# Windowed attention with a top-2 mixture of experts: a ring of nine slots for the values, three buffers for the turned values, and gate logits in half-width matmuls

## The chip, the cores and the metric

The kernel runs on one core of one Trainium2 chip. The metric is the device time of one execution in microseconds (us), from start to end on that core; lower is better. Times here are medians of several executions. One execution was also taken with the hardware profiler, and all rows below come from it.

## What is computed

The input is q, k and v of shape (8 batches, 8 heads, 576 positions, 64 features). Each position attends to itself and to the 63 positions before it. The attention output, seen as 4608 rows of 512 features, goes through a noisy top-2 gate and eight experts, each of two matmuls (512 to 1024, relu, 1024 to 512):

```python
mask = (rel >= 0) & (rel < window)              # window = 64
scores = np.where(mask, scale * q @ k.T, -1e9)
attn = softmax(scores);  x = attn @ v           # x: 4608 rows of 512
logits = x @ w_gate
noisy = logits + np.log1p(np.exp(x @ w_noise)) * noise
top2 = the two largest of the 8 experts, with softmax weights
out[row] += weight * (relu(x[row] @ w1[e]) @ w2[e])   # for both experts
```

All is in float32. The kernel never multiplies the attention output by the gate matrices. It multiplies v by them first, and lets the attention average the results: the gate logits of a key are 16 more value columns beside its 64 features.

## The kernel before, in words

**Two phases.** The attention phase has 36 steps, numbered j (NT = 36). Step j is block i = j // 4 of 64 positions of a pair of batches bp = j % 4. The expert phase follows, expert by expert; its first matmuls begin while the last steps of attention still run. The loop over j (lines 1104 to 1162) is written out by hand, and that order is the order of every engine's queue: nothing is rescheduled. Each engine works its own queue in order, and so does SyncE's queue, which issues the transfers.

**One step of the loop.** In the order of the code, with the engine that does it:
- `norm_a(j-3)` (lines 385 to 389): ScalarE copies the sums of the softmax (L388), VectorE takes the reciprocal (L389).
- `scores(j)` (L318; L320 in the first four steps): TensorE, 16 matmuls in 64x64 tiles of the array.
- `soft_a(j)` (L328): ScalarE copies a part of the scores into the tile `t`. In the first four steps GpSimd fills `t` instead (L330).
- `soft_b(j-1)` (L346): ScalarE takes the exponential and writes `p`.
- `pv(j-2)` (L378): TensorE, 32 matmuls in 64x64 tiles (16 in the first four steps), with the values of this block and of the block before. Then SyncE is told to load the values of step j+2 (`load_v`, L131).
- `place_slots(j-2)` (L608): TensorE, a few small bf16 matmuls of the routing.
- `norm_b(j-3)` in two halves (L399): ScalarE, eight scaled copies.
- `soft_max(j)`, `soft_max2(j)` (L336, L341, L342): VectorE merges the scores and takes the maximum, GpSimd subtracts it.
- `transp(j-1)` (L354): TensorE turns `p`, four transposes.
- `logits(j)` (lines 282 to 288): TensorE, the gate logits of the 128 keys of step j; then SyncE is told to load the turned values of step j+2 (`load_vt`, L137).
- `apply_mask(j-1)` (L359): VectorE.
- `logits_copy(j)` (lines 290 to 295): ScalarE moves the logits from PSUM beside the values.
- `gate(j-3)` (L416), and a share of the routing's small instructions, which come from a list on VectorE, ScalarE and GpSimd.

**The values.** `VW` (line 112) is one tile for each of the four pairs of batches, with two slots, i % 2. A slot holds four groups of value columns, which a transfer brings, and a fifth group with the gate logits, which ScalarE writes. `pv(j)` reads the slots of steps j and j-4. The load for step j+4 writes the slot that `pv(j)` reads as the block before. GpSimd zeroes the fifth groups once (L185).

**The turned values.** `VT` (L136) has two buffers. The load for step j+2 takes the buffer that `logits(j)` reads.

**The logits.** For each of four groups q of 128 rows of turned values, one matmul takes 128x128 weights (64 keys of each of two heads) and 64 moving columns, of which each half of the keys needs 32. The copy takes the right 32 for each half of the partitions, so there are two of it:

```python
nc.tensor.matmul(p[:, q * 64:q * 64 + 64], lhsT=x[:, q, :], rhs=wgx_sb[:, g], ...)
for a in range(2):                      # L292
    nc.scalar.activation(VW[bp][h, i % 2, 4, ...], VG[h, 0]...[:, :, a], AF.Copy)
```

**The start.** GpSimd works through masks, the zeroing of L185 and the constants of the routing (lines 428 to 458 and 637) in order, and only then fills `t` for step 0 (L330).

Of the kernel before, what the change touches and what calls it, by code (L numbers as in the profile page):

```python
# [8 lines left out]
F32 = mybir.dt.float32  # L9
# [4 lines left out]
AF = mybir.ActivationFunctionType  # L14
# [6 lines left out]
NP = B // 2  # L21
# [67 lines left out]
def tile_kernel(ctx, tc, qT, kT, vx, vT, wgx, noise, w1, w2, out):  # L89
    nc = tc.nc  # L90
# [14 lines left out]
    acon = at.enter_context(tc.tile_pool(name="acon", bufs=1))  # L105
    ld = at.enter_context(tc.tile_pool(name="ld", bufs=2))
    wk = at.enter_context(tc.tile_pool(name="wk", bufs=2))
# [1 line left out]

    KW = acon.tile([128, NP, 2, H, 64], F32)  # L110

    VW = [acon.tile([128, 2, 5, 2, 4, 17], F32, name=f"vw{j}") for j in range(NP)]
    QC, VT = {}, {}

    def load_q(j):
# [12 lines left out]

    def load_v(j):
        i, bp = divmod(j, NP)  # L130
        nc.sync.dma_start(VW[bp][:, i % 2, 0:4], vx[bp, i])  # L131


    def load_vt(j):
        i, bp = divmod(j, NP)
        VT[j] = ld.tile([128, 4, 128], F32, name="vt", bufs=2)  # L136
        nc.sync.dma_start(VT[j], vT[bp, i])  # L137

    for j in range(2):
# [1 line left out]
    wgx_sb = acon.tile([128, 2, 64], F32)  # L141
    nc.sync.dma_start(wgx_sb, wgx)
    load_vt(0)
    load_v(0)
    load_vt(1)
    load_qk(2)
    load_v(1)
    load_k(3)

# [3 lines left out]
    idle = ps.tile([128, 512], F32, name="ps_g")  # L153
# [19 lines left out]
    nc.vector.tensor_scalar(mcur, mprev, -1.0, 1.0, op0=OP.mult, op1=OP.add)  # L173

    maskT = acon.tile([128, 2, 2, 64], F32)
    other = acon.tile([128, 2, 64], F32)
    o3 = ones.rearrange("p (u r) -> p u r", u=2)
    nc.gpsimd.affine_select(maskT[:, 0], o3, pattern=[[0, 2], [1, 64]], base=0, channel_multiplier=-1,
                            compare_op=OP.is_ge, fill=0.0)
# [2 lines left out]
    nc.vector.tensor_copy(maskT[64:128, 0], other[64:128])  # L182
    nc.vector.tensor_scalar(maskT[:, 1], maskT[:, 0], -1.0, 1.0, op0=OP.mult, op1=OP.add)
    for v in VW:
        nc.gpsimd.memset(v[:, :, 4], 0.0)  # L185


    noise_sb = consts.tile([128, NT, E], F32)
# [88 lines left out]
        return lag([(w2s[:, f], W2["h"][:, f], W2["l"][:, f]) for f in (0, 4, 1, 5, 2, 6, 3, 7)])  # L277


    VG = idle[:, 0:256].rearrange("p (n c) -> p n c", n=1)  # L280

    def logits(j):
        p = VG[:, 0]
        x = VT.pop(j)
        for u in range(2):
            for g in range(2):
                q = u * 2 + g
                nc.tensor.matmul(p[:, q * 64:q * 64 + 64], lhsT=x[:, q, :], rhs=wgx_sb[:, g], start=True, stop=True)

    def logits_copy(j):  # L290
        i, bp = divmod(j, NP)
        for a in range(2):  # L292
            h = slice(a * 64, a * 64 + 64)
            nc.scalar.activation(VW[bp][h, i % 2, 4, :, :, 0:16].rearrange("p u (g x) e -> p (u g) x e", x=2),
                                 VG[h, 0].rearrange("p (k a x e) -> p k a x e", a=2, x=2, e=16)[:, :, a], AF.Copy)

    ST, T, P, TP, PT, XT = {}, {}, {}, {}, {}, {}

# [67 lines left out]
    def pv(j):  # L366
        i, bp = divmod(j, NP)
        o = aps.tile([128, 2, 512], F32, name="ps_o", bufs=2)
        OT[j] = o
        PO[j] = o[:, :, 0:340].rearrange("p a (k d) -> p a k d", d=85)  # L370
        pt, v = PT.pop(j), VW[bp]
        for g in range(2):
            for x in range(2):
                for w in range(2 if i else 1):
                    for a in range(2):
                        for u in range(2):
                            pa = slice(a * 64, a * 64 + 64)
                            nc.tensor.matmul(PO[j][u * 64:u * 64 + 64, a, g * 2 + x, :],  # L378
                                             lhsT=pt[pa, w, u * 2 + g, x * 64:x * 64 + 64],
                                             rhs=v[pa, (i + w) % 2, :, u, g * 2 + x, :],  # L380
                                             start=(w == 0), stop=(w == 1 or not i))
        if j + NP < NT:
            load_v(j + NP)
# [64 lines left out]
    for k in (1, 2, 4, 8, 16, 32):  # L448
        n = min(k, NT - k)
# [654 lines left out]
    for j in range(NT + 3):  # L1104
# [17 lines left out]
        if W1G // 2 - 4 <= j < W1G // 2 + 4:  # L1122
            k = j - W1G // 2 + 4
# [5 lines left out]
        ahead(2)  # L1129
        drain(rate(1))  # L1130
        on(pv, j - 2)
        on(place_slots, j - 2)
        if PACED <= j < NT - 3:
# [12 lines left out]
        on(transp, j - 1)  # L1146
        ahead(2)
        on(logits, j)
        if j < NT - 2:
            load_vt(j + 2)  # L1150
        blanks(j)
        on(norm_b, j - 3, 1)
        on(apply_mask, j - 1)
        drain(rate(2))
        on(logits_copy, j)
        ahead(2)
        on(gate, j - 3)
# [14 lines left out]
    d, z, v, y = ([mps.tile([128, 512], F32, name=f"ps_{x}{q}") for q in range(k)] for x, k in zip("dzvy", (2, 3, 1, 1)))  # L1172
# [188 lines left out]
```

## Time and profile before

| what | us |
|---|---|
| median of 3 runs (lowest, highest) | 998.04 (997.68, 999.22) |
| the profiled execution | 997.35 |
| its span, first to last instruction | 995.3 |
| busy in the span: TensorE | 956.3 |
| VectorE | 689.9 |
| ScalarE | 525.9 |
| GpSimd | 320.1 |

The profiled execution is 0.69 us under the median. A busy time is the time in which the engine had at least one instruction at work. TensorE's matmuls overlap each other, so TensorE may be counted busy while it does less than it could. PE is TensorE's matmuls and PEld its weight loads, DVE is VectorE, ACT ScalarE, POOL GpSimd, and SPq the queue on SyncE. An arrow such as `L354 <- ACT p L346` names what ended a wait; `<- issue` means that the profile shows nothing that the engine waited for. A float32 matmul of the code appears as two records on PE and two on PEld.

### The profile page before, as it was taken

The numbers are of one execution on the slowest core, as the hardware profiler recorded it, in microseconds if no ns is written. First come the engines' busy times: TensorE is split into PE (matmuls) and PEld (weight loads), VectorE is DVE, ScalarE is ACT, GpSimd is POOL, SyncE is SP. The second block draws the span as 40 slices with busy tenths as digits, with TensorE's granted clock in tenths as the row PEclk, the third lists the DMA queues.
The fourth block names the chain that finished last, engine by engine and source line by source line (L and its number), as shares of the span: only waits on it lengthen the run. The fifth ranks groups of instructions, "written<-read, shape, count | busy, mean of one in ns | idle before, by whom it ended". The sixth has DMA issues, their size and how long they took to land. (4 is left out here: it accounts for less than half of the span.)

```text
span 995.3 us, 21900 instructions
## 1 busy us (share of the span) xinstructions
PE 956.3 (96%) x8408; PEld 858.2 (86%) x8408; DVE 689.9 (69%) x1728; ACT 525.9 (53%) x1346; POOL 320.1 (32%) x442
## 2 busy tenths in 40 slices
PE   8788888999999999999999999999999999999996
PEld 8777787888879888989898989898989898989895
DVE  5688898763786777767766786668666867686730
ACT  4888877522455545544554455445544554455531
POOL 5346546122322414040414141413131323241303
PEclk9999999999999999999999999999999999999999
DMA  9989997894649456854584458454945494647304
GB/s 326 365 270 314 287 294 273 271 263 119 153 89 267 81 130 132 252 73 120 116 265 70 125 115 267 60 134 87 283 63 143 73 266 89 149 93 206 48 1 56
DMA packets 107810, 168.93 MB, mean 170 GB/s; under 512 B 13424, under 2 KB 57712, under 8 KB 105904
## 3 DMA queue, kind: packets, MB, share of 16 engines
q1 hardware_dynamic: 90544, 126.96, 41.7%
q0 software_dynamic: 17152, 40.48, 21.9%
q8 instruction: 68, 1.11, 0.5%
q14 instruction: 46, 0.38, 0.1%
HBM read 110.08 MB, written 57.32 MB: 168 GB/s over the span
## 5 line engine op out<-in xcount | busy, mean ns | idle before, releaser
L966 POOL DMA_INDIRECT out_dram<-xg,los x70 | 111.9, 1598 | 427.5 <-ACT xh L774 124.3
L900 ACT ACTIVATE hb<-tq 128x288 fp32r<-128x288 f32 (+1 forms) x168 | 76.9, 458 | 143.9 <-DVE tq L919 143.7
L1038 PE MATMUL ps_d<-w2h,hb 128*128 128x512 f32 x392 | 152.9, 390 | 0.0
L1039 PE MATMUL ps_d<-w2l,hb 128*128 128x512 f32 x392 | 152.8, 390 | 0.0
L1040 PE MATMUL ps_d<-w2h,hb 128*128 128x512 f32 x392 | 152.7, 390 | 0.0
L919 DVE TENSOR_TENSOR tq<-ps_z,tq 128x288 f32<-128x288 f32 (+1 forms) x168 | 79.2, 472 | 89.0 <-PE ps_z L890 88.5
L888 PE MATMUL ps_z<-xh,WH 128*128 128x288 f32 (+1 forms) x448 | 137.5, 307 | 0.9
L889 PE MATMUL ps_z<-xl,WH 128*128 128x288 f32 (+1 forms) x448 | 135.2, 302 | 0.0
L890 PE MATMUL ps_z<-xh,WL 128*128 128x288 f32 (+1 forms) x448 | 135.2, 302 | 0.0
L904 DVE SCALAR_TENSOR_TENSOR hb<-tq,hb 128x320 fp32r<-128x320 f32 (+2 forms) x168 | 75.6, 451 | 37.5 <-ACT hb L900 35.2
L888 PEld LDWEIGHTS ps_z<-xh,WH 128*128 128x128 f32 x448 | 84.0, 188 | 5.5 <-DVE tq L919 3.7
L1040 PEld LDWEIGHTS ps_d<-w2h,hb 128*128 128x128 f32 x392 | 73.6, 188 | 15.6
L1038 PEld LDWEIGHTS ps_d<-w2h,hb 128*128 128x128 f32 x392 | 73.6, 188 | 14.0
L1039 PEld LDWEIGHTS ps_d<-w2l,hb 128*128 128x128 f32 x392 | 73.6, 188 | 13.8
L889 PEld LDWEIGHTS ps_z<-xl,WH 128*128 128x128 f32 x448 | 84.1, 188 | 1.1
L890 PEld LDWEIGHTS ps_z<-xh,WL 128*128 128x128 f32 x448 | 84.1, 188 | 0.0
L698 POOL DMA_INDIRECT xg<-xrows,lxs x70 | 69.0, 986 | 23.2 <-issue 22.6
L782 ACT ACTIVATE xh<-tq 128x512 fp32r<-128x512 f32 (+1 forms) x70 | 42.7, 610 | 61.9 <-DVE tq L778 60.5
L235 DVE TENSOR_TENSOR WL<-ws,WH 128x512 fp32r<-128x512 f32 x112 | 67.2, 615 | 6.6 <-ACT WH L243 6.5
L399 ACT ACTIVATE x<-ps_o,r 128x80 f32<-128x80 f32 x288 | 67.0, 350 | 7.5 <-DVE r L389 7.2
L378 PE MATMUL ps_o<-vw,pt 64*64 64x85 f32 x2176 | 49.9, 235 | 12.7 <-issue 8.2
L342 POOL TENSOR_TENSOR t<-t,mx 128x512 f32<-128x512 f32 x36 | 38.8, 1078 | 70.8 <-DVE mx L341 49.2
(242 smaller groups left out, 2347.0 us busy)
## 6 DMA issues: line engine op xcount, KB each, us to landing
ws<-in_w_dram SPq DMA_DIRECT2D x14, 2048.0 KB, 11.5
xs<-xg SPq DMA_DIRECT2D x63, 256.0 KB, 3.4
vw<-in_vx_dram SPq DMA_DIRECT2D x36, 272.0 KB, 4.5
out_dram<-zero SPq DMA_DIRECT2D x38, 256.0 KB, 4.6
qc<-in_qT_dram SPq DMA_DIRECT2D x36, 256.0 KB, 4.8
KW<-in_kT_dram SPq DMA_DIRECT2D x36, 256.0 KB, 4.9
vt<-in_vT_dram SPq DMA_DIRECT2D x36, 256.0 KB, 4.6
xrows<-x SPq DMA_DIRECT2D x36, 256.0 KB, 4.9
```

What stands on the lines that cost most here:

```text
L235: eng.tensor_tensor(l, x, h.bitcast(F32), op=OP.subtract)
L698: nc.gpsimd.indirect_dma_start(out=XG[e, c, q][:m], out_offset=None, in_=X[:DUMP + seen.get((e, c), NT) * 128], in_offset=bass.IndirectOff ...
L888: nc.tensor.matmul(p[:, :n], lhsT=WH[:, a, k, w], rhs=xh[:, b, k, :n], start=first and k == 0, stop=False, **free)
L889: nc.tensor.matmul(p[:, :n], lhsT=WH[:, a, k, w], rhs=xl[:, b, k, :n], start=False, stop=False, **free)
L890: nc.tensor.matmul(p[:, :n], lhsT=WL[:, a, k, w], rhs=xh[:, b, k, :n], start=False, stop=(k == 1), **free)
L900: nc.scalar.activation(hh[:, f, a:b], src, AF.Relu)
L904: nc.vector.scalar_tensor_tensor(hl[:, f, a:m], src[:, :m - a], 0.0, hh[:, f, a:m].bitcast(F32), op0=OP.max, op1=OP.subtract)
L919: nc.vector.tensor_tensor(t, a[:, :n], t, op=OP.add)
L966: s = nc.gpsimd.indirect_dma_start(out=out[:(2 + seen.get((e, c), NT)) * 128], out_offset=bass.IndirectOffsetOnAxis(ap=LT[e, c][1][q][:m], ...
L1038: nc.tensor.matmul(p, lhsT=h, rhs=w2h[:, f, :], **a)
L1039: nc.tensor.matmul(p, lhsT=h, rhs=w2l[:, f, :], start=False, stop=False)
L1040: nc.tensor.matmul(p, lhsT=l, rhs=w2h[:, f, :], **b)
```

## The change

The values get nine tiles of one slot each, used in turn by j. The turned values get a third buffer. Each logits matmul is cut in two: 64 keys as weights (128x64) and the 32 columns that they need, written to the half of the partitions where those keys belong; one copy then moves all of it. The small mask `other`, used once at the start, moves into a buffer of `t`. The program uses 4,256 more bytes of each partition (one slot more of 2,720, one turned buffer more of 2,048, less 512 for `other`).

```diff
-    VW = [acon.tile([128, 2, 5, 2, 4, 17], F32, name=f"vw{j}") for j in range(NP)]
+    VW = [acon.tile([128, 5, 2, 4, 17], F32, name=f"vw{j}") for j in range(2 * NP + 1)]
...
-        nc.sync.dma_start(VW[bp][:, i % 2, 0:4], vx[bp, i])
+        nc.sync.dma_start(VW[j % len(VW)][:, 0:4], vx[bp, i])
...
-        VT[j] = ld.tile([128, 4, 128], F32, name="vt", bufs=2)
+        VT[j] = ld.tile([128, 4, 128], F32, name="vt", bufs=3)
...
-    other = acon.tile([128, 2, 64], F32)
+    other = wk.tile([128, 8, 64], F32, name="t")[:, 0:2]
...
     for v in VW:
-        nc.gpsimd.memset(v[:, :, 4], 0.0)
+        nc.gpsimd.memset(v[:, 4], 0.0)
...
-    VG = idle[:, 0:256].rearrange("p (n c) -> p n c", n=1)
+    VG = idle[:, 0:128].rearrange("p (n c) -> p n c", n=1)
...
-                nc.tensor.matmul(p[:, q * 64:q * 64 + 64], lhsT=x[:, q, :], rhs=wgx_sb[:, g], start=True, stop=True)
+                for a in range(2):
+                    h = slice(a * 64, a * 64 + 64)
+                    nc.tensor.matmul(p[h, q * 32:q * 32 + 32], lhsT=x[:, q, h], rhs=wgx_sb[:, g, a * 32:a * 32 + 32],
+                                     start=True, stop=True)
...
-        for a in range(2):
-            h = slice(a * 64, a * 64 + 64)
-            nc.scalar.activation(VW[bp][h, i % 2, 4, :, :, 0:16].rearrange("p u (g x) e -> p (u g) x e", x=2),
-                                 VG[h, 0].rearrange("p (k a x e) -> p k a x e", a=2, x=2, e=16)[:, :, a], AF.Copy)
+        nc.scalar.activation(VW[j % len(VW)][:, 4, :, :, 0:16].rearrange("p u (g x) e -> p (u g) x e", x=2),
+                             VG[:, 0].rearrange("p (k x e) -> p k x e", x=2, e=16), AF.Copy)
...
-        pt, v = PT.pop(j), VW[bp]
+        pt, v = PT.pop(j), [VW[(j - w * NP) % len(VW)] for w in range(2)]
...
-                                             rhs=v[pa, (i + w) % 2, :, u, g * 2 + x, :],
+                                             rhs=v[w][pa, :, u, g * 2 + x, :],
```

## Rows read from the trace of the kernel before

**Rows 1.** The page: busy time of each engine, and the queue of instructions.

```profile
PE 956.3 (96%) x8408; PEld 858.2 (86%) x8408; DVE 689.9 (69%) x1728; ACT 525.9 (53%) x1346; POOL 320.1 (32%) x442
...
q8 instruction: 68, 1.11, 0.5%
```

**Rows 2.** Busy time by stretch of the attention phase (stretch, length, each engine's busy us).

```profile
core 0: us, PE busy (x) PEld busy (x) DVE busy (x) ACT busy (x) POOL busy (x), PEclk, DMA share, GB/s
5.70:20.28 14.58, 13.27 (x269) 12.41 (x269) 7.74 (x12) 5.34 (x18) 7.94 (x20) 1.00 1.02 365
20.28:53.46 33.18, 27.08 (x693) 25.12 (x693) 20.57 (x33) 27.61 (x104) 12.23 (x15) 0.95 1.00 355
53.46:149.79 96.33, 83.25 (x2323) 75.36 (x2322) 86.55 (x217) 79.68 (x304) 52.39 (x60) 1.00 0.92 293
149.79:172.18 22.39, 17.64 (x460) 16.05 (x459) 18.64 (x50) 15.33 (x57) 14.81 (x18) 1.00 0.83 295
```

**Rows 3.** Timeline of TensorE over one step: start, length, instructions, idle before.

```profile
27.00 1.00 PE L288 MATMUL ps_g<-wgx_sb,vt 128*128 128x64 f32 x8
...
28.85 1.35 PE L378 MATMUL ps_o<-vw,pt 64*64 64x85 f32 x64
30.33 0.66 PE L354 MATMUL ps_t<-ident,p 128*128 128x128 f32 x4
30.82 1.00 PE L288 MATMUL ps_g<-wgx_sb,vt 128*128 128x64 f32 x8
31.75 0.45 PE L318 MATMUL ps_s<-KW,qc 64*64 64x128 f32 x8
```

**Rows 4.** Timeline of ScalarE over the same step.

```profile
28.04 0.56 ACT L294 ACTIVATE vw<-ps_g 64x128 f32<-64x128 f32 x2
...
29.16 0.60 ACT L328 ACTIVATE t<-ps_s 128x512 f32<-128x512 f32 x1 [0.36 <-PE ps_s L318]
29.66 0.62 ACT L346 ACTIVATE p<-t 128x512 f32<-128x512 f32 x1
30.18 1.85 ACT L399 ACTIVATE x<-ps_o,r 128x80 f32<-128x80 f32 x8
```

**Rows 5.** Waits of TensorE (total us, times, longest): two from 20.28:53.46, the last from 53.46:180.

```profile
PE ps_o L378 <- issue: 4.3, 3, 2.9
PE ps_t L354 <- ACT p L346: 1.6, 3, 0.7
...
PE ps_o L378 <- issue: 3.8, 6, 1.6
```

**Rows 6.** Waits of SyncE's queue from 5 to 175 us: its three largest.

```profile
SPq L137 <- PE ps_g L288: 20.0, 24, 2.0
SPq L131 <- PE ps_o L378: 14.7, 14, 1.9
SPq L131 <- PE ps_o L608: 10.0, 8, 2.0
```

**Rows 7.** TensorE's matmuls by form, 5 to 20 us: count, busy us, mean ns.

```profile
L288 PE MATMUL ps_g<-wgx_sb,vt 128*128 128x64 f32 x31 | 3.9, 268 | 0.0
L320 PE MATMUL ps_s<-KW,qc 64*64 64x64 f32 x128 | 3.0, 237 | 0.6 <-DVE t L336 0.6
...
L378 PE MATMUL ps_o<-vw,pt 64*64 64x85 f32 x64 | 1.6, 235 | 0.0
```

**Rows 8.** Timeline of TensorE where 64x64 tiles are followed by the whole array.

```profile
102.10 1.41 PE L378 MATMUL ps_o<-vw,pt 64*64 64x85 f32 x64
103.44 0.25 PE L608 MATMUL ps_o<-xc 128*128 128x80 bf16 x2
```

**Rows 9.** Timeline of TensorE in the expert phase: two neighbouring whole-array matmuls.

```profile
700.13 0.29 PE L890 MATMUL ps_z<-xh,WL 128*128 128x288 f32 x1
700.26 0.30 PE L888 MATMUL ps_z<-xh,WH 128*128 128x288 f32 x1
```

**Rows 10.** The start: the zeroing on GpSimd, and VectorE's first merge.

```profile
2.24 1.11 POOL L185 MEMSET vw<- 128x272 f32 x4
...
8.35 0.72 DVE L336 COPY_PREDICATED t<-mcur,ps_s 128x512 f32<-128x512 uint32 x1 [4.05 <-POOL t L330]
```

## The prediction

> **What bounds the kernel now.** I began with the page's busy times. TensorE is busy for 956.3 of 995.3 us [rows 1], so 39.0 us of idle time are all that waits can give back; more must come from less work on TensorE. The table by stretch shows where that idle time lies: 1.3, 6.1, 13.1 and 4.8 us in the four stretches [rows 2], 25.2 us together, all in the attention phase. The change edits that phase alone. The expert phase is TensorE's almost without a gap, so an earlier end of attention should move the whole end.
>
> Inside attention the bound changes. From 53 to 150 us VectorE is busy for 86.55 of 96.33 us, TensorE for 83.25 and ScalarE for 79.68 [rows 2]: three engines near their limit, the heaviest in front. From 20 to 53 us VectorE has 20.57 of 33.18 us and isn't the limit. There the timeline shows a chain [rows 3, 4]. Logits start at 27.00 and the next ones at 30.82, a step of 3.82 us. ScalarE waits for the scores (L328 at 29.16, after 0.36 us idle), then makes `p` (L346, 29.66 to 30.28), the transposes start at 30.33, the logits at 30.82, the next scores at 31.75. So scores, L328, L346, transposes and logits follow one another, while `pv` runs beside the two ScalarE instructions. Logits are on this chain, and ScalarE's copy L294 stands ahead of L328 in its queue.
>
> **The transfers: nothing.** SyncE's queue waits 20.0 us for logits at the load of turned values, and 14.7 and 10.0 us after `pv` at the load of values [rows 6]. The third buffer and the ninth slot take these waits away: each load then takes a place that was read a step earlier. I cost this at 0. The waits that it ends are the queue's own, and the list of TensorE's waits names no transfer that matters; a load issued two steps ahead has over 7 us of cover at 3.82 us a step. Next in the queue come the store (for L399) and the load of q (for the scores). The cover would be gone only if the transfer engines fell behind; they show a busy share of 0.92 to 1.02 in the first three stretches [rows 2], so earlier issue spreads the traffic but can't add to it much. `other` in a buffer of `t` adds no wait: its reader ends some 7 us before step 1 fills that buffer again.
>
> **The start: 0.3 us lost.** Four memsets of 272 columns took 1.11 us [rows 10], 0.28 us each. Now there are nine of 136, with 1,224 columns for 1,088. At the old price by column this is 0.14 us more, at the old price by instruction 1.4 us more. I take 0.3, nearer to the first, since each has half the columns. It lies on the path: VectorE waits 4.05 us for the fill that comes last in this queue [rows 10].
>
> **The logits on TensorE: 0.2 us a step.** Today eight records take 1.00 us, the last of them 0.268 [rows 3, 7], so they start 0.105 us apart. From the last one to the next scores it is 0.93 - 0.73 = 0.20 us [rows 3], about 0.1 more than a record: that is what leaving the whole array for 64x64 tiles costs. The other way, 64 `pv` records start 0.019 us apart ((1.41 - 0.235)/63), and L608 follows the last by 0.165 [rows 7, 8]: about 0.15. A switch therefore costs 0.1 to 0.15 us, and the change adds one: whole array to two halves ahead of the logits (there is one behind them already).
>
> Then 16 records in two halves of the array, which no row shows. The nearest are the 64x64 scores of the first steps with 64 moving columns: 128 records in 3.0 us over four steps, so 0.75 us for 32, starting (0.75 - 0.237)/31 = 0.0165 us apart [rows 7]; four tiles at once make a round of 0.066. Two halves make eight rounds: 7 x 0.066 = 0.46 us to the last start. From the transposes to the next scores we get 0.49 + 0.12 + 0.46 + 0.20 = 1.27 us, against 31.75 - 30.33 = 1.42 now. That saves 0.15; since only 32 columns stream, half of that row's, I take 0.2. The ends: all records at the pace of `pv`, 15 x 0.019 = 0.28, saves 0.33; all sixteen one behind the other at today's 0.105 (1.58 us) costs 0.97 more.
>
> **The copy on ScalarE: 0.28 us a step.** Two copies take 0.56 us [rows 4]; one over all partitions has the same columns in each, so 0.28. This counts only where ScalarE's queue is the limit, as from 32 to 53 us, where the splitting of weights is added to it. I don't add it to the 0.2: both shorten the same step.
>
> **The instruction supply: 0.6 us lost.** TensorE has gaps in the middle of `pv` that end on nothing shown: 4.3 us in 3 and 3.8 us in 6, the longest 2.9 [rows 5]. The queue of instructions moved 1.11 MB for 2 x 8,408 records of TensorE [rows 1], 66 bytes each; I read these gaps as waits for the program. The change adds 36 x 8 = 288 matmul records and as many loads of weights, 576. The four stretches hold 7,490 records of both kinds and 8.1 us of gaps, 1.1 ns each: 0.6 us. [...]
>
> **The sum.** Steps 1 to 3: 3 x 0.2 = 0.6. Steps 4 to 10 (20 to 53 us): 7 x 0.2 = 1.4. Steps 11 to 31 (53 to 150 us): VectorE leaves (96.33 - 86.55)/21 = 0.47 us a step, unevenly, so some steps gain 0.2 or more and some nothing; I take 0.12, 2.5 in all. Steps 32 to 35: 4 x 0.2 = 0.8. Together 5.3, less 0.3 and 0.6: 4.4 us. The profiled execution took 997.35 us, so 993.0; the median of the runs is 0.7 above it: **993.7 us**.
>
> **The rivals.**
> *The gain is swallowed* (about 997): VectorE sets all of steps 11 to 35, and gaps in the supply take what the early steps give: 2.0 - 0.3 - 0.6 = 1 us. For it: VectorE's 90% in the longest stretch. Against: TensorE waits there for ScalarE and for the supply too, not for VectorE alone.
> *The two halves queue up* (about 1003, slower): the sixteen records run one behind the other at a round's 0.066: 15 x 0.066 + 0.12 + 0.20 + 0.49 = 1.80 us against 1.42, so 0.38 more. On the ten early steps that is 3.8, on the 25 later ones half of it, 4.7, of which the shorter copy returns some 4.5 (25 steps, two thirds of 0.28); with the start and the supply this is 4.9 slower than 997.35, so some 1003 on the median. It decides once records start more than (1.42 - 0.81)/15 = 0.041 us apart. At the full 0.105 it is 0.97 a step, over 20 us. Against: in 64x64 tiles, four loads of weights and four matmuls fit in 0.066 us [rows 7], and two of the four share their rows of the array. [...]
> *The waits were the point* (about 990): if the queue's waits delay loads or stores that hold others up in a way the list hides, part of the 44.7 us [rows 6] comes back besides; I give 4 us more.
>
> **How the numbers follow.** The forecast 0.6, swallowed 0.2, queueing 0.12, waits 0.08. About 0.2% (2 us) is what a measurement of this kernel can tell from no change. Faster by more: forecast and waits, 0.68. Within: the swallowed case, 0.2. Slower: 0.12. The range takes the forecast with its bounds: below, 0.33 a step (3 us more) and the 2.9 us gap gone, 988; above, no gain and one gap more, 999.5. Queueing is left out.
>
> **What would show it.** Logits: 16 records of 128x64 weights within about 0.6 us and 0.2 less from transposes to scores. L294: 36 copies for 72, about 0.28 us each. SyncE's waits on L288 and L378 gone, no engine gaining by that. The first fill of `t` 0.3 us later. Wider gaps of "issue" in `pv`, VectorE's share from 53 us on above 0.90. I am wrong if logits records start over 0.041 us apart, if TensorE's idle time in attention grows by as much as logits shrink, or if the expert phase starts earlier and the end doesn't move.

## The result and the profile after

The kernel after takes **1009.27 us** (median of 7 runs, 1002.28 to 1009.88) against 998.04 (7 runs) on the same chip: a ratio of 1.0104, 95% interval 1.0081 to 1.0127. The forecast was 993.7. The change makes the kernel slower, by about 10 us, and the whole range of the prediction lies below the result. Times vary a little from chip to chip (the kernel before had medians from 998.0 to 1000.8), so every experiment below is given as a ratio to the kernel before on its own chip.

The profiled execution of the kernel after took 1009.88 us. Its page, busy times and queue of instructions, against [rows 1]:

```profile
PE 954.5 (95%) x8696; PEld 848.6 (84%) x8696; DVE 691.2 (69%) x1728; ACT 514.0 (51%) x1310; POOL 320.2 (32%) x447
...
q8 instruction: 71, 1.16, 0.5%
```

TensorE is busy for 1.8 us less and ScalarE for 11.9 us less, as meant, and the span grew from 995.3 to 1008.2 us. So most of the loss is waiting. The next rows say where it begins: the last `pv` on TensorE's timeline, first in the kernel before, then in the kernel after.

```profile
179.10 1.41 PE L378 MATMUL ps_o<-vw,pt 64*64 64x85 f32 x64
```

```profile
191.50 1.41 PE L379 MATMUL ps_o<-vw,pt 64*64 64x85 f32 x64
```

12.4 of the 12.9 us are lost before the attention phase ends; the expert phase is only shifted. The busy times from 5 us to just behind that `pv`, before and then after (columns as in [rows 2]):

```profile
5.00:180.30 175.30, 149.90 (x3905) 136.53 (x3904) 139.13 (x328) 132.52 (x496) 90.49 (x115) 0.99 0.92 305
```

```profile
5.00:192.70 187.70, 148.04 (x4193) 127.08 (x4192) 139.67 (x328) 120.65 (x460) 90.47 (x116) 0.96 0.86 286
```

TensorE is busy for 1.9 us less and idle for 39.7 us instead of 25.4, 14.3 more. Its lists of waits over these two stretches (total us, times, longest) say for what, before and then after; [rows 5] were parts of the first:

```profile
PE ps_o L378 <- issue: 8.2, 9, 2.9
PE ps_t L354 <- ACT p L346: 5.0, 10, 0.7
...
PE ps_s L318 <- issue: 1.0, 1, 1.0
```

```profile
PE ps_o L379 <- issue: 11.9, 8, 3.5
PE ps_s L319 <- issue: 8.6, 8, 2.5
...
PE ps_g L290 <- issue: 4.0, 2, 2.3
PE ps_t L355 <- ACT p L347: 2.7, 5, 0.7
...
PE ps_t L355 <- issue: 1.3, 2, 1.1
```

The waits that end on nothing shown are 25.8 us, for 9.2; that is 16.6 more. The wait of the transposes for `p` fell from 5.0 to 2.7. And the waits no longer sit in `pv` alone: they are also ahead of scores, in the middle of the logits, and between two transposes. One step of TensorE's timeline with such a wait, and one without, against [rows 3]:

```profile
28.08 0.66 PE L290 MATMUL ps_g<-wgx_sb,vt 128*64 128x32 f32 x16
28.67 1.10 PE L319 MATMUL ps_s<-KW,qc 64*64 64x128 f32 x32
29.67 1.41 PE L379 MATMUL ps_o<-vw,pt 64*64 64x85 f32 x64
31.07 0.66 PE L355 MATMUL ps_t<-ident,p 128*128 128x128 f32 x4
31.66 0.48 PE L290 MATMUL ps_g<-wgx_sb,vt 128*64 128x32 f32 x9
33.74 0.42 PE L290 MATMUL ps_g<-wgx_sb,vt 128*64 128x32 f32 x7 [1.61 <-issue]
34.09 1.10 PE L319 MATMUL ps_s<-KW,qc 64*64 64x128 f32 x32
```

Nine of the sixteen logits records run, then TensorE stands still for 1.61 us, then the other seven run. They read the same tiles as the first nine, so their inputs were there. What they lacked was the program, as the next paragraph shows.

**The program comes in blocks.** The queue of instructions moved 1.16 MB in 71 packets, 16.3 KB each; with 17,392 records of TensorE (8,696 matmuls and as many loads) that is some 250 records to a packet. Counting all of TensorE's records in the trace in the order of their starts (its few semaphore and branch records too), one finds these gaps at whole multiples of 256 records from each other. This list is worked out from the records of the trace (gaps of the kernel after over 0.3 us from 20 to 110 us; a packet's start and landing are those of the instruction queue):

```
resume   gap   record        packet start   landing   landing to resume
21.83    0.69  193 + 2x256   19.46          20.38     1.45
33.74    1.61  193 + 4x256   31.35          32.35     1.39
45.04    2.49  193 + 6x256   42.51          43.41     1.63
50.61    1.39  193 + 7x256   48.30          49.24     1.37
75.51    0.92  193 + 12x256  73.31          74.27     1.23
81.37    1.93  193 + 13x256  79.19          80.13     1.24
86.93    1.67  193 + 14x256  84.67          85.55     1.38
97.13    1.11  193 + 16x256  94.12          95.69     1.44
103.67   2.35  193 + 17x256  101.44         102.38    1.29
```

18 of the kernel's 20 gaps over 0.15 us lie at such a block end, 23.9 of the 25.8 us, and there TensorE goes on 1.2 to 1.7 us after the block's packet has landed. In the kernel before it is 7 gaps of 10, 7.5 of the 9.2 us. The 2.9 us gap of the kernel before [rows 5] lies at record 193 + 6x256 too, with 1.29 us from landing to resumption. A step has 32 + 64 + 4 + 16 = 116 matmul records and as many loads, 232, where [rows 3] give 216; so a step uses up nine tenths of a block.

The clock loses something as well. Two stretches in the table by stretch: the first begins 1.2 us behind the gap that ends at 103.67, the second lies over the end of the longest gap, 3.5 us until 157.43:

```profile
104.90:109.00 4.10, 4.10 (x96) 3.35 (x86) 1.88 (x4) 2.86 (x10) 1.04 (x1) 0.58 0.54 136
...
156.10:163.00 6.90, 5.57 (x98) 4.99 (x102) 2.62 (x9) 0.51 (x3) 1.60 (x2) 0.51 0.70 235
```

In the second the granted clock is 0.51, and 98 matmuls fill 5.57 us; 32 records of scores, 1.10 us long at 34.09, take 1.98 there (from 161.09). In all, 13.7 us of attention ran at that level, against 3.4 in the kernel before; by estimate, half of the 10.3 us between them, that is at most 5.1 us more. Not all of it goes with the program: the last 3.4 us, from 173.2, follow two waits for VectorE's `pt` (1.3 and 1.8 us), and the ring alone (experiment 1) has 13.7 us at that level too.

### The profile page after: what moved, and what is told of

It is laid out like the page before. It is cut to its first block, busy times and chain, and to the rows that moved or that the text cites. A ratio compares the mean times of both kernels' runs of the same rounds, so it can differ in the third digit from the quotient of the medians.

```text
span 1008.2 us, 22389 instructions
## 1 busy us (share of the span) xinstructions
PE 954.5 (95%) x8696; PEld 848.6 (84%) x8696; DVE 691.2 (69%) x1728; ACT 514.0 (51%) x1310; POOL 320.2 (32%) x447
## 3 DMA queue, kind: packets, MB, share of 16 engines
q8 instruction: 71, 1.16, 0.5%
## 5 line engine op out<-in xcount | busy, mean ns | idle before, releaser
L379 PE MATMUL ps_o<-vw,pt 64*64 64x85 f32 x2176 | 53.1, 241 | 14.0 <-issue 11.9
```

## The experiments

Each is compared with the kernel before on its own chip. Four letters carry through the expectations: A (the number of TensorE's records: the program comes too slowly), B (traffic of the transfers delays the program), C (where the block ends happen to fall), D (which place in the step a block end has, and the pace there); every other letter belongs to the one experiment that names it. The waits come from one profiled execution each, and not each of these is typical: in the repeat of the logits alone it took 998.35 us, against a median of 1003.9; with 8 tiny matmuls 997.33 against 1002.57; with two buffers 1011.56 against 1006.4; with one copy 1001.72 against 999.51.

**1. The change in two.** First the ring, the third buffer and `other` alone, with the logits and copies of before:

```diff
...
-                for a in range(2):
-                    h = slice(a * 64, a * 64 + 64)
-                    nc.tensor.matmul(p[h, q * 32:q * 32 + 32], lhsT=x[:, q, h], rhs=wgx_sb[:, g, a * 32:a * 32 + 32],
-                                     start=True, stop=True)
+                nc.tensor.matmul(p[:, q * 64:q * 64 + 64], lhsT=x[:, q, :], rhs=wgx_sb[:, g], start=True, stop=True)
...
```

> The ring of nine and the third buffer alone, with the old full-width logits and two copies. Before is at 998, the whole change at 1009, and TensorE's gaps that end on nothing shown (taken to be waits for its program) grew from 9 to 26 us. Theory A (records): the 16 more records of a step eat the program faster; then this kernel has none of them and takes 998 to 999, gaps near 9 us. Theory B (traffic): loads issued earlier stand in front of the program's own transfers; then this kernel shows the loss already: 1004 to 1010, gaps over 15 us. Theory C (place): the loss hangs on where the ends of the program's blocks fall in a step; this kernel has the old records in the old places, so 998 to 999 too.

Then the half-width logits and the one copy alone, on the eight places and two buffers of before (the reverse edit, on the other kernel).

> The half-width logits and the single copy alone, with the old ring of eight and two turned buffers. Theory A (records): the loss is all here: 1006 to 1010, gaps over 20 us. Theory B (traffic): the logits give what was forecast for them, 992 to 996, gaps near 10 us. Theory C (place): as A for this kernel, 1006 to 1010; the shifted kernels tell it from A.

Measured: the ring alone 1.0017 (0.9996 to 1.0039), no loss that can be told from none. The logits alone 1.0055 (1.0034 to 1.0076). The waits of TensorE on nothing shown, 5 to 180 us, the ring alone first:

```profile
PE ps_o L378 <- issue: 9.0, 13, 2.0
PE ps_s L318 <- issue: 1.1, 2, 0.7
```

```profile
PE ps_o L379 <- issue: 9.4, 13, 1.5
PE ps_g L290 <- issue: 5.6, 4, 1.9
PE ps_s L319 <- issue: 4.7, 5, 1.8
```

10.1 us with the ring, as before (9.2); 19.7 in these three lines with the logits. The gaps belong to the part that adds records, though that part takes work off TensorE. B, with 992 to 996, falls. A fits in kind and not in size: it wanted 1006 to 1010 and over 20 us of waits here, and the median is 1003.84, about half of the loss; experiment 7 takes up the rest.

**2. The block ends shifted.** Both kernels get 100 records more at the start, in the same time (fewer warming matmuls, 64 small ones in their place), so that every block end falls at another place of its step.

```diff
-    warm(10)
+    warm(3)
...
+    for _ in range(64):
+        nc.tensor.matmul(idle[:, 384:400], lhsT=early, rhs=early[:, 0:16], start=True, stop=True)
```

> The kernel before with about 100 more records on TensorE in the warm-up at the start, in the same time (three warm matmuls and 64 tiny ones for ten), so that the ends of the program's blocks fall in other places of every step. Theories A and B: 997 to 1000, gaps 7 to 12 us. Theory C: moves by 4 us or more, either way.

> The changed kernel with the same 100 records more in the warm-up. Theories A and B: 1006 to 1011, gaps over 20 us. Theory C: moves by 4 us or more from 1009, and could come out under 1000.

Measured: 0.9993 (0.9975 to 1.0012) and 1.0074 (1.0052 to 1.0096). The kernel before doesn't mind (8.4 us of waits on nothing shown). The kernel after seems 3 us better than at first, but unchanged it also gave 1.0078 in experiment 7. Its waits are 17.2 us, less than the 20 that A and B expected, and they sit elsewhere in the step, nearly all in `pv`:

```profile
PE ps_o L383 <- issue: 15.1, 16, 3.3
```

So most of the loss is no accident of where the ends fell, and C isn't its cause; whether up to 3 us hang on the place, this pair can't say.

**3. Records by themselves.** The kernel before with 8 tiny matmuls (16 records, 8 columns each) between scores and `pv` in every step, and then with 16 of them.

```diff
         on(scores, j)
+        if j < NT:
+            tiny()
...
+    def tiny():
+        for _ in range(4):
+            for x in range(2):
+                px = slice(x * 64, x * 64 + 64)
+                nc.tensor.matmul(idle[px, 384:392], lhsT=ones_b[0:64, 0:64], rhs=ones_b[0:64, 0:8], start=True, stop=True)
```

> The kernel before with eight tiny bf16 matmuls (64x64 weights, 8 columns, result never read) after the scores of each step: 16 records more, as many as the half-width logits add, and some 0.1 to 0.2 us of work on TensorE, 3 us in all. Theory A (records): the number of records is what costs, so gaps on nothing shown rise from 9 to between 15 and 22 us, and the time to 1003 to 1010. Rival A2 (density): the loss comes because the half-width logits run through faster than the old ones, which had given the program time to arrive; then gaps stay at 8 to 12 us and the time is 999 to 1002.

> The kernel before with 16 tiny matmuls (32 records) a step behind the scores, double the 16 records that cost 3.5 us. If the supply is a pace per record (theory A), the price per record rises once the step is longer than its supply: 8 to 16 us in all, 1006 to 1014, and waits on 'issue' of 20 us or more. If the 16 records cost their own execution (theory K, some 0.1 us a step), twice that: 1004 to 1006, waits on 'issue' as before.

Measured: 1.0035 (1.0012 to 1.0058) and 1.0071 (1.0049 to 1.0094). The second has no steepening. Its waits from 5 to 180 us, and two places of its timeline, with the tiny matmuls at L1059:

```profile
PE ps_o L378 <- issue: 12.9, 19, 2.2
```

```profile
101.37 0.37 PE L1059 MATMUL ps_g<-ones_b 64*64 64x8 bf16 x14
...
106.50 0.40 PE L1059 MATMUL ps_g<-ones_b 64*64 64x8 bf16 x16
```

The waits are 12.9 us, not the 20 or more that A asked for. Sixteen tiny matmuls run for 0.40 us, of which (0.40 - 0.17)/15 = 0.015 us each is pace (0.17 is the mean of one): 16 x 0.015 = 0.24 us a step, 8.6 in all, and 7.1 were lost. Theory K, that these records cost their own time, fits better. The first kernel's waits are 9.4 us, as A2 had them, though in an execution that was the fastest of its ten. So the bare number of records does not bring the gaps that A asked for, and a record has no fixed price: at this kernel's pace, 4.99 us a block (table below), 32 records take 0.62 us to arrive, and a step grew by 7.1/36 = 0.20 us. The kernel before had room for part of them: 11 of its 24 blocks in that table began more than 1.7 us behind their landing. What the logits do is different: they add 16 records **and** shorten the step.

**4. Fewer records in the kernel after.** The logits matmuls are left out in the odd steps from 5 on.

```diff
         x = VT.pop(j)
+        if j > 4 and j % 2:
+            return
```

> The kernel after, with the eight logits matmuls left out in every odd step from 5 on (16 steps, 512 records; the copy stays and takes what lies there): the same number of records as the kernel before within some 70, ring, buffers and copy as after. Theory A (the supply of the program limits attention once records per step rise from 218 to 234): at or below the kernel before, 993 to 999, waits on 'issue' 5 to 180 us at most 13 us for 25.6. Rival G (it isn't the count but how the kernel after is arranged: the ring's addresses, the order of transfers, the copy): still 1004 to 1008, waits of 18 us or more. Note that TensorE also does less work here, some 0.6 us in each of 16 steps, so a time of 990 would be more than A needs.

Measured: 0.9991 (0.9968 to 1.0014), with these waits from 5 to 180 us:

```profile
PE ps_o L381 <- issue: 10.9, 18, 1.7
PE ps_s L321 <- issue: 3.6, 4, 1.3
```

14.5 us of waits for 25.8, a little over the 13 that A allowed, and the time where A had it. The test isn't clean: TensorE also has 16 x 0.6 = 9.6 us less to do, and 1009.3 less 9.6 is 999.7, the measured time, so the time doesn't speak against G (the arrangement alone). The waits do: ring, buffers and copy are those of the kernel after, and G wanted 18 us or more.

**5. Less traffic.** The loads of k and v are left out from step 9 on, in the kernel after and in the kernel before.

```diff
-        nc.sync.dma_start(KW[:, bp, i % 2], kT[bp, :, i])
+        if j < 9:
+            nc.sync.dma_start(KW[:, bp, i % 2], kT[bp, :, i])
...
-        nc.sync.dma_start(VW[j % len(VW)][:, 0:4], vx[bp, i])
+        if j < 9:
+            nc.sync.dma_start(VW[j % len(VW)][:, 0:4], vx[bp, i])
```

> The whole change, with the loads of k and of the values left out from step 9 on (the slots keep what earlier steps loaded, so the attention there is of other keys). Some 530 of 1,300 KB a step are gone. Theory B in its weaker form (the program's transfers queue behind the data, so the gaps need heavy traffic): gaps from 60 us on fall by more than half, attention ends before 184 us. Theory A alone (the records and their places, traffic or not): gaps stay within a quarter of the changed kernel's 25.6 us, attention ends at 189 to 194 us.

> The kernel before with the loads of k and v left out from step 9 on (steps 9 to 35 use what lies in those places): the control for the same cut on the kernel after, which came 13.3 us below it. Theory A (records: the kernel before is only just supplied in time, so a quicker fetch has little to give it): within 4 us below the kernel before, waits on 'issue' in attention 6 to 10 us for 9.2. Rival B (the traffic itself costs time in either kernel, by the transfers or the memory's ports, and the light version of after was faster for that alone): as much as on after, 10 us or more below, at 988 or less. If A holds, the two light versions stand within 3 us of each other, though the kernels stand 11 us apart.

Measured: 0.9974 (0.9955 to 0.9992) for the light version of after, 0.9960 (0.9942 to 0.9978) for that of before. For the kernel after, the weaker form of B came true and A alone fell: its last `pv` starts at 177.69 us, so attention ends before 184, and from 60 us on the gaps fall from 19.2 to 6.1 us. The control then stands beside it, as A expected: the same cut gave the kernel after some 10 to 13 us and the kernel before 4. The stretch from 53 to 150 us and TensorE's waits on nothing shown, first of the light after, then of the light before:

```profile
53.46:149.79 96.33, 82.39 (x2505) 70.15 (x2501) 86.85 (x218) 72.56 (x284) 54.00 (x61) 0.98 0.60 185
...
PE ps_o L381 <- issue: 5.0, 7, 1.2
PE ps_s L321 <- issue: 3.1, 5, 1.6
PE ps_g L292 <- issue: 2.2, 2, 1.9
```

```profile
53.46:149.79 96.33, 83.57 (x2348) 75.85 (x2340) 87.26 (x222) 79.35 (x303) 53.44 (x60) 1.00 0.62 184
...
PE ps_o L380 <- issue: 3.9, 5, 1.5
```

With the transfer engines at a share of 0.60 to 0.62, not 0.87 and 0.92, the gaps shrink in both kernels, in the kernel after from 25.8 to 10.7 and in the kernel before from 9.2 to 3.9. No other engine's work was touched. So the data's transfers delay the program, and that costs time mainly in the kernel that needs its program sooner. A and B don't exclude each other, as my expectations had it: both are part of the mechanism.

**6. The place of the block end in the step.** Half-width logits alone, and in each step as many tiny matmuls as put the next block end at a wanted place (up to 32, where the place is near): once right behind the logits, once three quarters through `pv`.

```diff
...
+    def fill(n):
+        n = n % 256
+        if n <= 64:
+            for q in range(n // 2):
+                px = slice(q % 2 * 64, q % 2 * 64 + 64)
+                nc.tensor.matmul(idle[px, 384:392], lhsT=ones_b[0:64, 0:64], rhs=ones_b[0:64, 0:8], start=True, stop=True)
...
+        elif j < NT:
+            fill(193 - 40 - recs[0])
         on(transp, j - 1)
```

(200 in place of 40 for the second; `recs` counts the records issued so far.)

> Half-width logits with the old ring and buffers, and up to 11 tiny bf16 matmuls ahead of the transposes of each step from 4 on, so many that the end of a 256-record block always falls right behind the logits, where the records ahead of it are the slow ones (logits, transposes, waits for ScalarE). Theory D (place and pace: a block is asked for when the one before has been read out, and TensorE stands still if the records that it still holds run out sooner than the next block comes): gaps fall from 20 to under 8 us, and the time to 990 to 998 though there is more work. If number alone counts (A): gaps 20 us or more, 1004 to 1009.

> The same as the kernel with block ends behind the logits, the same number of tiny matmuls within two a step, but the end of a block always falls three quarters through the value matmuls, where the 150 records ahead of it are the fastest of the step. Theory D: a gap of about 1 us in nearly every step, 25 us or more in all, and 1006 to 1025. Theory A: as the other, 1004 to 1009, gaps 20 us.

Measured: 1.0155 (1.0125 to 1.0185) and 1.0040 (1.0022 to 1.0057), in the opposite order to D. The waits, first with the ends behind the logits, then in `pv` (both from 5 to 180 us; all matmuls show as L160 here):

```profile
PE ps_g L160 <- issue: 20.1, 13, 3.2
```

```profile
PE ps_o L160 <- issue: 17.9, 24, 1.9
```

The waits moved to where the block ends were put. One of the first kind, ahead of the last of the sixteen logits records:

```profile
107.51 0.65 PE L160 MATMUL ps_g<-wgx_sb,vt 128*64 128x32 f32 x15
109.60 0.24 PE L160 MATMUL ps_g<-wgx_sb,vt 128*64 128x32 f32 x1 [1.44 <-issue]
```

Only the number of tiny matmuls, and with it the place of the 256th record, was set here. So this shows more directly than anything else that the gaps are waits for the next 256 records. With thirteen waits of 1.5 us in the mean the kernel loses 15 us; with 24 waits of 0.75 us it loses 4, though all waits on nothing shown are 23.0 us in the first and 20.1 in the second. A reason could be the chain: a wait between logits and scores lies on the way through scores, `p` and transposes; one inside `pv` lies beside the work on ScalarE, as the prediction read from [rows 3, 4]. But the first also has 30.7 us at the lower granted clock and the second 13.7, which by estimate, half of the 17.0 us between them, can make up to 8.5 of the 11 us between the profiled executions. So the place matters; by which of the two, these runs don't show. In the kernel before the gaps lie in `pv` (8.2 of 9.2 us); in the kernel after 13.9 of 25.8 us lie outside it.

**7. What the ring adds.** The first comparisons gave 1.0104 for all and 1.0055 for the logits alone, on different chips. Two kernels take back one half of the ring's part each, two repeat the ends on one chip.

```diff
-        VT[j] = ld.tile([128, 4, 128], F32, name="vt", bufs=3)
+        VT[j] = ld.tile([128, 4, 128], F32, name="vt", bufs=2)
```

> The kernel after with two buffers for turned values instead of three: that load again waits for the logits of two steps earlier. What the ring's part costs on top of the logits is 4 to 5 us (1.0055 for logits alone, 1.0104 for all). Theory H (the third buffer lets the loads of turned values run ahead and bunch with other traffic, which delays the program's fetch): 1004 +- 2. Rival I (the ring's nine slots do it): 1008 to 1010, unchanged. Rival C (each variant falls on its own pattern of block ends): anywhere from 1002 to 1010, with no row of waits that goes along.

The counterpart has three buffers and the new logits on the eight places of before:

> The kernel before with half-width logits, one copy and three buffers for turned values, but the old eight places for values (that load again waits for the outputs of the same step): the counterpart of the one with two buffers. Theory H (the third buffer): 1008 to 1010. Rival I (the ring of nine slots): 1004 +- 2, as the logits alone. Rival C (pattern of block ends): anywhere from 1002 to 1010, with both counterparts on the same side.

The kernel after unchanged, and the logits alone again:

> The kernel after, unchanged, beside the one with half-width logits alone on the same chip: whether the ring and the third buffer add anything. By the first comparisons 1.0104 and 1.0055, on other chips. If the ring adds (rival L): 4 us or more over the logits alone. If the two differ by the chip and by the execution (theory A, the logits carry it all): within 2 us of each other, both 1.005 to 1.010.

> Half-width logits with one copy alone, on the ring and buffers of before, beside the whole change on the same chip: 1003 to 1008 by either; what tells is the distance to the whole change (4 us or more: the ring adds; under 2 us: it doesn't).

Measured: two buffers 1.0047 (1.0022 to 1.0072), old places 1.0034 (1.0009 to 1.0058), all again 1.0078 (1.0051 to 1.0104), the logits again 1.0044 (1.0021 to 1.0067). The last two are 4.5 us apart in their medians, but their intervals overlap. Neither half of the ring's part adds anything by itself; both together may add some 3 to 5 us. H and I both fall, for each wanted the two half-way kernels some 4 us apart; what C said of them, that both fall on the same side, is so. L isn't settled. The repeat shows the same waits as the first profile of after:

```profile
PE ps_o L379 <- issue: 11.2, 11, 2.2
PE ps_s L319 <- issue: 7.6, 6, 2.4
PE ps_g L290 <- issue: 3.4, 3, 1.6
```

**8. The shorter copy by itself.** The kernel before, the second copy left out from step 5 on.

```diff
-        for a in range(2):
+        for a in range(2 if j < 5 else 1):
```

> The kernel before, with the second of the two copies of gate logits left out from step 5 on (31 copies of some 0.28 us less on ScalarE; the gate logits of half the keys are then stale): what the change's shorter copy is worth by itself, with TensorE's records as before. Theory A with my forecast's step (ScalarE's queue is on the chain in some steps, and the program still comes in time): 2 to 5 us below the kernel before. Rival J (a shorter step only meets the program's pace: at 218 records a step the supply already holds the kernel before to within a few us): within 1.5 us of it, with the waits on 'issue' up by about what ScalarE's chain gives, from 9.2 to 12 us or more.

Measured: 0.9985 (0.9968 to 1.0002), a gain of 1.5 us that can't be told from none; the waits on nothing shown rose from 9.2 to 13.2 us:

```profile
PE ps_o L378 <- issue: 9.4, 12, 2.4
PE ps_o L608 <- issue: 2.0, 1, 2.0
PE ps_s L318 <- issue: 1.8, 2, 1.2
```

The time and the sum of the waits are what J said, but the waits are not of the kind it meant. By the count of records only 8.5 of the 13.2 us lie at block ends, where the kernel before has 7.5 of 9.2; the other 4.7 us lie elsewhere, and what they wait for isn't shown. The profiled execution is also 2.2 us above its median. So the copy is worth little, but that the supply of the program takes its gain back isn't shown. This also says that a version with one copy and the old logits, which would beat both kernels if any part of the change did, has 1.5 us or so to gain. It wasn't tried, and no kernel that computes the whole thing came out faster than the one before.

**The blocks, side by side.** Worked out from the records of each trace, blocks of 256 records that begin between 20 and 150 us: mean time of a block, time from its first record to the start of the next block's packet (median), and how many blocks began within 1.7 us of their packet's landing, that is, waited for it or all but did. The last column is the part of the waits on nothing shown, over the whole of attention, that lies at block ends.

```
kernel                      block us   packet starts after   waited     at block ends, us
before                      5.48       2.54                  13 of 24    7.5
the ring alone              5.54       2.25                  11 of 24    6.0
one copy left out           5.42       2.32                  12 of 24    8.5
light before                5.35       1.18                   4 of 24    2.8
logits alone                5.30       2.59                  22 of 25   17.4
logits alone, again         5.09       2.49                  20 of 26   10.7
after                       5.34       2.83                  21 of 24   23.9
after, again                5.40       2.97                  23 of 25   22.1
after, half the logits      5.31       2.65                  18 of 25   12.3
light after                 4.98       2.23                  23 of 26   10.7
16 tiny matmuls             4.99       2.38                  23 of 26   12.0
```

In the kernel after, 2.83 us to the packet's start, 0.96 for the packet and some 1.4 to the first record make 5.2 us, and a block takes 5.34: nearly every block runs at the pace of its supply. 232 records at 256 in 5.34 us are 4.84 us a step, where the kernel before has 216 x 5.48/256 = 4.62 (a few records of the routing come on top in both; from transposes to transposes the steps measure 4.86 and 4.65). The light before needs 216 x 5.35/256 = 4.51 and rarely waits: that is about what the engines need. With the light after, the supply's pace is 4.98 us, so 4.51 us a step too.

The pace isn't the same everywhere: where nearly all blocks wait, it lies between 4.98 and 5.40 us. Traffic is a part of that, and it shows inside the kernels too. Take the 327 blocks of all 18 traces that began within 1.7 us of landing and sort them by the busy share of the transfer engines in the block's first 2 us. The next packet started after 1.65 us where the share was under 0.5 (median of 14 blocks), after 2.19 from 0.5 to 0.8 (43), after 2.60 from 0.8 to 1.02 (195), and after 3.11 above that (75). The 1.18 of the light before is not traffic alone: few of its blocks waited, and in a block that began later than its landing the next packet came earlier (in the kernel before 1.64 us into such blocks, 2.60 into the 13 others).

## Why the prediction was wrong

**The instruction supply is the step that failed.** I named the cause (the gaps in `pv` as waits for the program) and then priced it as 1.1 ns a record, 0.6 us, with one more gap of 2.9 us as the upper end. The waits on nothing shown grew by 16.6 us, nearly all of it at block ends (23.9 us for 7.5). The price was a mean over a phase in which 13 of 24 blocks began on the heels of their packet. In the kernel after 21 of 24 do. There a step can't be shorter than its records take to arrive, so a saving on TensorE turns into waiting: by that kernel's pace, 5.34/256 = 0.021 us a record, the sixteen records more are worth 0.33 us a step, against 0.24 us saved on the chain. That pace is no constant of the chip (4.98 to 5.40 us a block, and 0.20 us a step for 32 records in experiment 3), so this balance says why the gain was lost and doesn't give the ten.

The 12.4 us that attention lost add up from the rows: 16.6 more for the waits on nothing shown, 2.3 less for `p`, 1.9 less of busy time. The clock is inside the last: without its 5.1 us at most, TensorE would have been busy for up to 7.0 us less. One of my signs of being wrong came up: the idle time in attention grew by 14.3 us, more than the 36 x 0.24 = 8.6 by which the logits shrank.

The upper end doesn't follow from its own words either. No gain, 0.3 us at the start and one gap of 2.9 us are 998.05 + 3.2 = 1001.2, not 999.5; the result lies above that too.

**The logits on TensorE: right.** The sixteen records don't queue up: they take 0.66 us, (0.66 - 0.223)/15 = 0.029 us from start to start with 0.223 for one (the median of them), under the 0.041 at which the rival of queueing decides. Logits to scores takes 28.67 - 28.08 = 0.59 us, transposes to logits 31.66 - 31.07 = 0.59, together 1.18 for 1.42: 0.24 saved where 0.2 was forecast. So the rival of queueing fell in its mechanism, though the sign came out as it had it. Each of the sixteen has a load of its own over all rows, and they start 0.029 us apart while one is shown as 0.223 long.

**The copy: right in size.** On ScalarE's timeline there is one for two, of 0.28 us, against [rows 4]:

```profile
28.79 0.28 ACT L295 ACTIVATE vw<-ps_g 128x128 f32<-128x128 f32 x1
```

I hadn't added it to the 0.2. By itself it is worth 1.5 us in experiment 8, and the interval there doesn't rule out no gain at all.

**The start: right.** Nine memsets for four, on GpSimd and in VectorE's first merge, against [rows 10]: 0.31 us more, and 0.30 us later.

```profile
2.23 1.42 POOL L185 MEMSET vw<- 128x136 f32 x9
```

```profile
8.65 0.72 DVE L337 COPY_PREDICATED t<-mcur,ps_s 128x512 f32<-128x512 uint32 x1 [4.04 <-POOL t L331]
```

**The transfers: right for the ring alone.** SyncE's waits for logits and for `pv` [rows 6] are gone, and the queue now waits at the next load, as foreseen, for q behind the scores:

```profile
SPq L118 <- PE ps_s L319: 30.2, 21, 5.6
SPq L403 <- ACT vw L295: 10.3, 6, 3.0
```

No engine gained by it, and the ring alone gave 1.0017. I had thought of the transfers only as cover for their own data, and not of the program's packets, which started later where the transfer engines were busier (1.65 us into a block that had waited at a share under 0.5, 3.11 above 1.02).

**VectorE as the bound from 53 us on: no longer.** It has 82.97 of 96.33 us there, less than the 86.55 of [rows 2]; the stretch does less work in the same time, on all engines:

```profile
53.46:149.79 96.33, 75.69 (x2310) 64.63 (x2307) 82.97 (x209) 68.18 (x265) 50.16 (x57) 0.98 0.87 278
```

So of the three rivals none named the result. *Swallowed* was nearest in mechanism: it had the supply take back a part of what the early steps give, 0.6 us, and left a gain of 1 us. *Queueing* was nearest in number (1003) by a cause that the trace refutes.

**What stays open.** What decides when a block's packet starts wasn't found, beyond that busier transfer engines went with a later start (1.65 to 3.11 us into the block); nor was the reason why 16 tiny matmuls, with more records, have a faster pace (4.99 us a block) than the kernel after (5.34). Whether ring and third buffer together add 3 to 5 us to the logits isn't settled, and what would do it neither: the packets start later with both (2.83, 2.97) than with either (2.60 and 2.62) or none (2.59, 2.49), but with the old logits the ring shows no such thing (2.25).

## What to carry to other kernels

Where a profile shows TensorE waiting for nothing, and the waits lie at equal distances in records (256 here), count the records of a step against the time in which a block of the program arrives before you price a change. Here a step of 232 records met a block of 256 in 5.34 us, and the fewer and larger logits matmuls beat the more and smaller ones, which do less work (the logits alone: a ratio of 1.0055). The 0.24 us a step saved on the path of data was worth little while the program set the pace (16.6 us more of waits on nothing shown), and data moved meanwhile slowed the program (10.7 us of these waits without the loads of k and v from step 9 on, 25.8 with them). Don't price such a limit by an average over a phase in which only half of the blocks meet it. And before you call a wait a wait for the program, count whether it lies at a block end: in experiment 8 a third of such waits didn't.

## What the runs showed of the hardware

- The queue of instructions brought packets of 16,384 bytes, 68 of them before and 71 after, with 16,816 and 17,392 records of TensorE; 18 of the 20 gaps over 0.15 us in the attention of the kernel after lie at whole multiples of 256 records from each other. There a packet took 0.96 us (median from 20 to 150 us), and TensorE went on 1.2 to 1.7 us after it had landed. Putting the 256th record elsewhere put the wait elsewhere (experiment 6).
- Busier transfer engines went with a later start of the next packet: 1.65 us into a block that had waited at a share under 0.5, 2.60 at 0.8 to 1.02. With the loads of k and v left out the kernel after had 2.23 for 2.83 us, and 10.7 us of waits for 25.8.
- A float32 matmul showed as two matmul records and two loads, so it took four of the 256 (four matmuls of the logits are eight records in [rows 3], and the page counts as many loads as matmuls, 8,408 [rows 1]). Sixteen tiny bf16 matmuls of 64x64 weights ran 0.015 us apart.
- Float32 records of column halves (128x64 weights, 32 moving columns) started 0.029 us apart, where whole-array records of 64 columns stood 0.105 us apart [rows 3, 7].
- The granted clock fell to 0.51 in stretches of 3.4 and 6.8 us, behind a gap of 2.35 us and over the end of one of 3.5 us, though the mean over the phase is 0.96; in the longer one 32 records of scores took 1.98 us, 1.10 elsewhere.
